# Second layer: squares behind the roundings, a tile's eight transpositions in one run, residual terms last in the second product; the weight conversion quiet in more ticks

## The chip, the cores and the metric

The kernel runs on one core of a Trainium2 chip. The metric is device time in microseconds (us) of one execution. Names of engines are those of the profile: PE (matmul) with PEld (its weight loads), DVE (vector), ACT (scalar), POOL (GpSimd), SP (whose queue starts the DMAs).

## The reference

Three layers follow one another. Attention over 2 batches x 8 heads x 768 tokens x 64 (a local window of 96 and 8 global keys, with a linear distance penalty) gives x of 1536 tokens x 512. A first layer mixes 4 experts of 512 to 1024 to 512. The second layer is the one that most of the change is in:

```python
h = x @ w_in                                  # 1536 x 1024
e = np.exp(h - np.max(h, axis=-1, keepdims=True))
sm = e / (np.sum(e, axis=-1, keepdims=True) + 1e-09)
solu = h * sm
mu = np.mean(solu, axis=-1, keepdims=True)
var = np.mean((solu - mu) ** 2, axis=-1, keepdims=True)
ln = (solu - mu) / np.sqrt(var + 1e-06) * g_ln
return ln @ w_out                             # 1536 x 512
```

All tensors are float32. The second layer's weights arrive as 64-bit words and are converted on the chip.

## The kernel before, in words

**Numbers in two halves.** A float32 value is multiplied as two parts: a rounded one (fp32r; "hi", made on ACT or POOL by a copy) and its residual ("lo", made by a subtraction on DVE or POOL). A product takes three matmuls for each 128 of depth: hi x hi, hi x lo, lo x hi.

**First layer.** `moe` goes through 8 half experts (`he`). From `he` = 2 on, one half expert is: `tail_groups` (the last 512 tokens, in seven groups of products numbered i = 1, 2, 6, 5, 7, 3, 4, of 256 columns), four groups of second products (`run`), `paired_groups` (1024 tokens, seven groups in the order 1, 2, 6, 5, 7, 4, 3, of 512 columns), and twice four groups of second products. The seven groups are a seven-product scheme for a two by two block product. In it the result of a first group is copied out of PSUM by ACT (L644 in the tail, L725 in the pairs) before the next group adds into the same bank, and DVE adds copy and bank (L652, L730) before ACT applies the ReLU (L608).

**Ticks.** Behind each group `st.tick()` writes small pieces of side work into the engines' streams: splitting of weights (L296, L304), loads, and the conversion of the second layer's weights. A conversion unit is a list of steps (`conv_steps`): load, two groups of integer operations on DVE, `two`/`both` (DVE, then the rounding on ACT, L201; for half of the units a scaling on ACT before it, L200), `parts` (L204) and a store to `w_dram` (L425). Units of the first 16 also make sums of quarter matrices and round and store those (`form`, L432 to L435: rounding on ACT, residual on DVE or POOL). With `quiet=True` a tick does no conversion step. Every engine takes its stream strictly in the order written, so a conversion step that waits holds back what stands behind it on its engine.

**Second layer.** `solu_layer` works on 12 tiles of 128 tokens. Tiles 0 and 1 get their hidden values by `g3`, the pairs after that by `pair(p)`, which again is seven groups of six matmuls in the order 1, 5, 6, 3, 7, 2, 4, with copies on ACT behind 1, 5 and 6 (L967; group 6 adds into the bank that group 1 was copied from) and additions on DVE (L970) behind 3, 7 and 2. Then come, for each tile: `largest` (DVE, L979), `powers` (ACT, L984), `products` (DVE, L989 to L994), and `squares` (ACT, L998, then two small POOL operations, L999 and L1000, that give the factor `rstd` for the output). The result must be turned so that its 1024 values lie across partitions: for tiles 0, 1, 10 and 11 by PE (`turned`: eight 128 x 128 transpositions, L1037; roundings on ACT, L1039; residuals on DVE, L1040), for the others by DVE and a trip through DRAM (`blocks`, `rounded`, `rests`). `g4(t)` is the second product, 24 matmuls in the order hi, hi, lo for each of eight slices (L1053), and its copy out (L1058) goes to `out`. Two PSUM tiles "o" are used in turn by `g4` and by `turned` for tiles 0 and 1; for tiles 10 and 11 `turned` uses the two halves of one tile.

The order of all of this is the order in which the Python code writes it; there is no planner, and the waits on semaphores follow from the data.

Of the kernel before, what the change touches and what calls it, by code (L numbers as in the profile page):

```python
# [25 lines left out]
NSLOT = NT // 128  # L26
# [25 lines left out]
def kernel(ctx, tc, ep, qk, vp, nn, pr, wall, w64, gl, out):  # L52
    nc = tc.nc
# [154 lines left out]
    def stream(arm):  # L208
# [5 lines left out]
        st = St()  # L214
# [179 lines left out]
        def conv_steps():  # L394

            n = st.next_conv
            st.next_conv += 1
            c, role, (j, h) = n, -1, (0, 0)
            if n < 16:
                role, (j, h) = n % 4, divmod(n // 4, 2)  # L400
                c = 2 * (2 * j + (1, 0, 5, 4)[role]) + h
            raw = st.cvp.tile([128, 256], I64, tag="r64", name=f"{arm}r64", bufs=2)
            af, cf = (st.cvs[:, n % 2, 256 * i:256 * i + 256] for i in range(2))
            one, two, parts, halves = from_f64(raw, af, cf)
            k0, k1 = (st.kk[:, i] for i in range(2))
            v = nc.vector

            def load():
                nc.sync.dma_start(out=raw, in_=w64[c])

            def both():
                two(gt[:, (c - 16) // 2:(c - 16) // 2 + 1] if c >= 16 else None)
                if role == 0:
                    nc.scalar.copy(k0, af)
                elif role == 1:
                    v.tensor_tensor(out=cf, in0=k0, in1=af, op=ALU.subtract)
                    nc.scalar.copy(k1, cf)
                elif role == 2:
                    v.tensor_tensor(out=cf, in0=af, in1=k0, op=ALU.subtract)
                    v.tensor_tensor(out=k1, in0=af, in1=k1, op=ALU.subtract)  # L420
                elif role == 3:
                    v.tensor_tensor(out=cf, in0=af, in1=k1, op=ALU.subtract)

            def store(p, h):
                nc.sync.dma_start(out=w_dram[p, :, :, 256 * h:256 * h + 256], in_=halves.bitcast(F32))  # L425
                st.stored += 1

            def ends():
                parts()
                store(c // 2, c % 2)  # L430

            def form(m, t, eng):  # L432
                nc.scalar.copy(halves[:, 0], t)
                eng.tensor_tensor(out=halves[:, 1], in0=t, in1=halves[:, 0].bitcast(F32), op=ALU.subtract)
                store(16 + 2 * m + j, h)  # L435

            forms = {1: [(0, cf, v)], 2: [(2, cf, v)], 3: [(3, cf, v), (1, k1, nc.gpsimd)]}.get(role, ())
            steps = [load, nothing, one, both, ends]
            for x in forms:
                steps += [nothing, lambda x=x: form(*x)]  # L440
            return n % 2, steps
# [358 lines left out]
    def moe(st, first_blocks):  # L800
# [28 lines left out]
        for he in range(1, NHE):  # L829
            if he == 1:  # L830
                yield from run(he, (2 * HALF, 512), False)
                st.tail_forms(st.now + 1)
            else:
                h3 = [], []
                for i in st.tail_groups(he, h3):
                    yield 0, 0.0
                    if i in (2, 5, 3, 4):
                        st.tick(i == 2, i != 2, 1)
                yield from run(he, (2 * HALF, 512), False, h3)
            h1, h2 = ([[None] * 4, [None] * 4] for _ in range(2))  # L840
            for i in st.paired_groups(he, h1, h2):
                yield 0, 0.0
                st.tick(quiet=i == 7)
            yield from run(he, (0, HALF), False, h1)
            yield from run(he, (HALF, HALF), True, h2)

# [23 lines left out]
    def solu_layer(st, arm):  # L870
# [13 lines left out]
        with ExitStack() as es:  # L884
# [127 lines left out]
            def halves(t, g):  # L1012
                return [x[:, g] for x in sets[t % 2]]
# [16 lines left out]

            def turned(t, pts):
                tt = t_b[t % 2]
                for g in range(2):
                    pt = pts(g)
                    for c in range(4):
                        f0 = (4 * g + c) * 128
                        nc.tensor.transpose(pt[:, 128 * c:128 * c + 128], tt[:, f0:f0 + 128], ident)  # L1037
                    th, tl = halves(t, g)
                    nc.scalar.copy(th, pt)  # L1039
                    nc.vector.tensor_tensor(out=tl, in0=pt, in1=th.bitcast(F32), op=ALU.subtract)  # L1040
                tts[t] = [[x.rearrange("p (c q) -> p c q", c=4) for x in halves(t, g)] for g in range(2)]

# [3 lines left out]
            def g4(t, f0=0, f1=8, c0=0, n=512):  # L1046
                if f0 == 0:
                    outs[t] = out_bank(t)[:, :n]
                ps = outs[t]
                for fc in range(f0, f1):  # L1050
                    th, tl = tts[t][fc // 4]
                    for i, (a, b) in enumerate(((th, 0), (th, 1), (tl, 0))):
                        nc.tensor.matmul(ps, lhsT=a[:, fc % 4], rhs=wo[fc][:, b, c0:c0 + n],  # L1053
                                         start=(fc == 0 and i == 0), stop=(fc == 7 and i == 2))
                if f1 < 8:
                    return
                o = o_b[t % 2][:, c0:c0 + n]
                nc.scalar.activation(o, ps, AF.Copy, scale=rstd[t])  # L1058
                b, i = SLOTS[t]
                nc.sync.dma_start(out=out[b * S + 128 * i:b * S + 128 * i + 128, c0:c0 + n], in_=o)  # L1060
# [3 lines left out]
            def soft_pair(p, old=None):  # L1064
                t0, t1 = 2 * p, 2 * p + 1
                largest(t0)
                powers(t0)
                if old is not None:
                    rounded(old)
                largest(t1)  # L1070
                powers(t1)
                for t in (t0, t1):
                    products(t)
                    if t == t0 and old is not None:
                        rests(old)
                    squares(t)
                    if p < last:
                        blocks(t)

            forms(1)  # L1080
            for t in range(2):
                g3(t)
                largest(t)
                powers(t)
                products(t)
                squares(t)
            load_form(3)
            forms(2)
            turned(0, out_bank)
            pair(1, {7: [lambda: turned(1, out_bank)]})  # L1090
            soft_pair(1)
            for p in range(1, last):
                if p + 2 <= last:
# [2 lines left out]
                g4(2 * p - 1)  # L1096
                pair(p + 1, {7: [lambda: rounded(2 * p), lambda: rests(2 * p)]})
                soft_pair(p + 1, 2 * p + 1)
            tail = bank()
            g4(NSLOT - 4)  # L1100
            turned(NSLOT - 2, lambda g: tail[:, g])
            g4(NSLOT - 3)
            g4(NSLOT - 2, 0, 4)
            tail = bank()
            turned(NSLOT - 1, lambda g: tail[:, g])
            g4(NSLOT - 2, 4, 8)
            g4(NSLOT - 1, 0, 8, 0, 256)
            g4(NSLOT - 1, 0, 8, 256, 256)
# [599 lines left out]
```

## Time and profile before

| | us |
|---|---|
| median of 3 runs | 752.25 |
| the runs | 752.08 to 753.03 |
| the profiled execution | 752.41 |
| its span | 750.6 |
| PE busy in the span | 723.8 (96%) |
| DVE, POOL, ACT busy | 494.3, 317.2, 311.0 |

The profile shows one execution. A row of the timeline gives the start, the busy time, the engine, the line, the operation with output and input tile, the count, and in square brackets how long the engine sat idle before it and who ended that wait. The span starts at 0; the second layer begins at 598 us. A matmul's busy time is modelled and overlaps the next; the distance between starts is what one costs.

### The profile page before, as it was taken

What the parts mean: (1) busy time and instruction counts of PE and PEld (TensorE: products, weight loads), DVE (VectorE), ACT (ScalarE), POOL (GpSimd) and SP (SyncE); (2) the same over time, 40 slices, a digit from 0 to 9 for tenths busy, and PEclk for the clock granted to TensorE, in tenths of its full rate; (3) what the DMA queues carried; (4) which work ended last, traced back from release to release, by engine and by line L of the source; (5) the groups of instructions that cost most, each with busy time, mean ns of one, the idle gap of its engine ahead of it and who ended that gap; (6) DMA issues with size and microseconds to landing.
All of it is one profiled execution on the core that took longest, in us unless ns stands there. A gap on an engine that the chain in (4) does not pass through costs nothing.

```text
span 750.6 us, 11200 instructions
## 1 busy us (share of the span) xinstructions
PE 723.8 (96%) x3887; PEld 599.6 (80%) x3887; DVE 494.3 (66%) x1083; ACT 311.0 (41%) x707; POOL 317.2 (42%) x378
## 2 busy tenths in 40 slices
PE   8999999999999999999999999999999979999966
PEld 6687877888788788889888888888988868778755
DVE  6787867638776776677769579677435546666640
ACT  4776756423522433233243253424324233444431
POOL 5600034574873074255226306422741484666000
PEclk9999999999999999999999999999999999999989
DMA  6733421312433234134143333323104840344401
GB/s 215 186 101 108 121 67 43 99 56 84 141 113 98 93 105 127 56 128 120 63 141 103 95 98 116 111 88 94 57 18 181 311 178 35 107 140 141 141 15 48
DMA packets 56979, 81.44 MB, mean 108 GB/s; under 512 B 5840, under 2 KB 34768, under 8 KB 56912
## 3 DMA queue, kind: packets, MB, share of 16 engines
q1 hardware_dynamic: 56352, 80.19, 33.7%
q8 instruction: 33, 0.54, 0.3%
q10 hardware_dynamic: 560, 0.43, 0.2%
q14 instruction: 34, 0.28, 0.1%
HBM read 60.65 MB, written 19.95 MB: 107 GB/s over the span
## 4 chain that ended last, share of the span: by engine, by line
PE 79%; DVE 11%; ACT 4%; issue 3%; DMA 1%; POOL 1%; DVEq 0%; ACTq 0%; SPq 0%; POOLq 0%
PE fg L570 34%; PE fg L720 15%; PE fg L639 6%; PE fo L1053 6%; PE fg L541 5%; PE fh L963 5%; PE x L1287 2%; PE sps L1183 2%; PE pt L1265 2%; DVE fhl L1028 1%; DVE scr L991 1%; ACT fhh L608 1%; DVE fg L652 1%; DVE fnm L979 1%; DMA v<-in_vp_dram 1%
## 5 line engine op out<-in xcount | busy, mean ns | idle before, releaser
L570 PE MATMUL fg<-fhh,wV 128*128 128x512 f32 (+1 forms) x800 | 243.5, 384 | 0.4
L570 PEld LDWEIGHTS fg<-fhh,wV 128*128 128x128 f32 x800 | 148.3, 188 | 33.7 <-issue 3.3
L570 PE MATMUL fg<-fhl,wV 128*128 128x512 f32 (+1 forms) x400 | 149.3, 381 | 0.0
L570 PEld LDWEIGHTS fg<-fhl,wV 128*128 128x128 f32 x400 | 75.0, 188 | 14.7 <-DVE fhl L556 0.3
L608 ACT ACTIVATE fhh<-fg 128x512 fp32r<-128x512 f32 x80 | 47.7, 599 | 66.3 <-DVE fg L730 36.5
L304 POOL TENSOR_TENSOR wR<-kr,wR 128x512 fp32r<-128x512 f32 (+1 forms) x28 | 29.0, 1060 | 79.7 <-ACT wR L296 79.7
L578 DVE TENSOR_TENSOR fg<-fg,pb 128x512 f32<-128x512 f32 x60 | 41.7, 694 | 28.0 <-PE fg L570 28.0
L720 PE MATMUL fg<-xt,fwS 128*128 128x512 f32 x252 | 58.3, 389 | 0.0
L583 POOL TENSOR_TENSOR scr<-scr,kr 128x512 f32<-128x512 f32 x24 | 31.0, 1292 | 61.7 <-DVE kr L582 61.7
L609 DVE SCALAR_TENSOR_TENSOR fhl<-fg,fhh 128x512 fp32r<-128x512 f32 x80 | 53.9, 687 | 3.4 <-ACT fhh L608 1.8
L720 PE MATMUL fg<-xh,wR 128*128 128x512 f32 x168 | 54.3, 391 | 1.3 <-DVE fg L730 1.3
L720 PEld LDWEIGHTS fg<-xt,fwS 128*128 128x128 f32 x252 | 47.3, 188 | 9.8
L730 DVE TENSOR_TENSOR fg<-kr,fg 128x512 f32<-128x512 f32 x42 | 28.7, 693 | 28.0 <-PE fg L720 20.9
L1053 PE MATMUL fo<-xt,fhh 128*128 128x512 f32 (+1 forms) x156 | 46.8, 385 | 0.0
L1243 ACT ACTIVATE p<-p,mn 128x256 f32<-128x256 f32 x68 | 33.8, 498 | 27.4 <-DVE mn L1238 27.4
L579 DVE TENSOR_TENSOR scr<-fg,scr 128x512 f32<-128x512 f32 x60 | 41.5, 692 | 2.0
L541 PE MATMUL fg<-xh,wR 128*128 128x512 f32 (+1 forms) x128 | 39.5, 373 | 0.0
L201 ACT CAST fr<-fcvs 128x256 fp32r<-128x256 f32 x32 | 11.9, 373 | 65.5 <-DVE fcvs L197 60.5
L720 PEld LDWEIGHTS fg<-xh,wR 128*128 128x128 f32 x168 | 31.5, 188 | 8.7 <-DVE fg L730 2.2
L582 DVE TENSOR_TENSOR kr<-fg,pb 128x512 f32<-128x512 f32 x24 | 16.6, 691 | 29.6 <-PE fg L570 27.8
L304 POOL TENSOR_TENSOR fwS<-kr,fwS 128x512 fp32r<-128x512 f32 x28 | 35.7, 1296 | 0.7 <-ACT fwS L296 0.7
L1053 PEld LDWEIGHTS fo<-xt,fhh 128*128 128x128 f32 x156 | 29.5, 196 | 5.4
(270 smaller groups left out, 1545.7 us busy)
## 6 DMA issues: line engine op xcount, KB each, us to landing
w_dram<-fr SPq DMA_DIRECT2D x48, 256.0 KB, 2.4
kr<-in_wall_dram SPq DMA_DIRECT2D x42, 256.0 KB, 2.8
fr<-in_w_dram SPq DMA_DIRECT2D x32, 256.0 KB, 2.7
pb<-p_dram SPq DMA_DIRECT2D x22, 256.0 KB, 3.7
v<-in_vp_dram SPq DMA_DIRECT2D x10, 512.0 KB, 3.5
kr<-t_dram SPq DMA_DIRECT2D x32, 128.0 KB, 2.9
frawt<-in_wall_dram SPq DMA_DIRECT2D x14, 256.0 KB, 2.8
wR<-w_dram SPq DMA_DIRECT2D x6, 512.0 KB, 4.0
```

Source lines behind the costliest of these rows:

```text
L304: e.tensor_tensor(out=w[:, 1], in0=t, in1=w[:, 0].bitcast(F32), op=ALU.subtract)
L541: nc.tensor.matmul(ps[:, :n], lhsT=w[:, a, k], rhs=b[:, k, cols], start=(k == 0 and i == 0), stop=(k == 3 and i == 2))
L570: nc.tensor.matmul(ps[:, :n], lhsT=w[:, a, k], rhs=b[k], start=(i == 0), stop=(i == 11))
L578: nc.vector.tensor_tensor(out=ps[:, :n], in0=ps[:, :n], in1=pg, op=ALU.mult)
L579: nc.vector.tensor_tensor(out=a, in0=ps[:, :n], in1=a, op=ALU.add)
L608: nc.scalar.activation(th, src, AF.Relu)
L609: residuals.append(lambda: nc.vector.scalar_tensor_tensor(out=tl, in0=src, scalar=0.0, in1=th.bitcast(F32), op0=ALU.max, op1=ALU.subtract))
L639: nc.tensor.matmul(ps[:, q_ * q:q_ * q + q_], lhsT=w[:, a, j], rhs=x[b][j], start=(opens and q == j == m == 0), stop=(j == 1 and m == 2), ...
L720: nc.tensor.matmul(ps, lhsT=w[:, a, j], rhs=x[b][j], start=(i in (1, 2, 5) and j == 0 and m == 0), stop=(j == 1 and m == 2), skip_group_ch ...
L963: nc.tensor.matmul(ps[i], lhsT=left[i][x][j], rhs=right[i][j][:, y], start=(i in (1, 5, 2) and j == m == 0), stop=(j == 1 and m == 2), ski ...
L1053: nc.tensor.matmul(ps, lhsT=a[:, fc % 4], rhs=wo[fc][:, b, c0:c0 + n], start=(fc == 0 and i == 0), stop=(fc == 7 and i == 2))
L1243: nc.scalar.activation(p[:, a], p[:, a], AF.Exp, bias=mn[:, a:a + 1], scale=-1.0, accum_out=st_rs[u][:, a, 0:1])
```

## The change

Six edits, of which none alters what is computed.

1. `form` rounds on the engine that also makes the residual (DVE for 12 of the 16, POOL for 4) and not on ACT.
2. `tail_groups`: the tick behind group 2 is quiet too (the three others were already). `paired_groups`: the tick behind group 5 is quiet as well as the one behind group 7.
3. `turned` writes its eight transpositions in one run and then both roundings; the residuals are a function of their own, `turned_rests`.
4. `g4` takes the 16 matmuls with hi on the left first and then the 8 with lo.
5. The beginning of the second layer is written in another order: roundings of tile 0 come before the exponentials of tile 1, and the squares of tiles 0 and 1 stand behind groups 3 and 7 of the first pair.
6. In the last pair `squares` goes behind the roundings of its tile.

```diff
             def form(m, t, eng):
-                nc.scalar.copy(halves[:, 0], t)
+                eng.tensor_copy(out=halves[:, 0], in_=t)
...
                     if i in (2, 5, 3, 4):
-                        st.tick(i == 2, i != 2, 1)
+                        st.tick(i == 2, True, 1)
...
-                st.tick(quiet=i == 7)
+                st.tick(quiet=i in (5, 7))
...
             def turned(t, pts):
                 tt = t_b[t % 2]
-                for g in range(2):
-                    pt = pts(g)
-                    for c in range(4):
-                        f0 = (4 * g + c) * 128
-                        nc.tensor.transpose(pt[:, 128 * c:128 * c + 128], tt[:, f0:f0 + 128], ident)
+                both = [pts(g) for g in range(2)]
+                for f in range(8):
+                    nc.tensor.transpose(both[f // 4][:, 128 * (f % 4):128 * (f % 4) + 128], tt[:, 128 * f:128 * f + 128],
+                                        ident)
+                for g, pt in enumerate(both):
+                    nc.scalar.copy(halves(t, g)[0], pt)
+                return both
+
+            def turned_rests(t, both):
+                for g, pt in enumerate(both):
                     th, tl = halves(t, g)
-                    nc.scalar.copy(th, pt)
                     nc.vector.tensor_tensor(out=tl, in0=pt, in1=th.bitcast(F32), op=ALU.subtract)
...
-                for fc in range(f0, f1):
-                    th, tl = tts[t][fc // 4]
-                    for i, (a, b) in enumerate(((th, 0), (th, 1), (tl, 0))):
-                        nc.tensor.matmul(ps, lhsT=a[:, fc % 4], rhs=wo[fc][:, b, c0:c0 + n],
-                                         start=(fc == 0 and i == 0), stop=(fc == 7 and i == 2))
+                terms = [(fc, i) for k in ((0, 1), (2,)) for fc in range(f0, f1) for i in k]
+                for fc, i in terms:
+                    a = tts[t][fc // 4][i // 2]
+                    nc.tensor.matmul(ps, lhsT=a[:, fc % 4], rhs=wo[fc][:, i % 2, c0:c0 + n],
+                                     start=(fc == i == 0), stop=(fc == 7 and i == 2))
...
                     products(t)
                     if t == t0 and old is not None:
                         rests(old)
-                    squares(t)
                     if p < last:
+                        squares(t)
                         blocks(t)
...
-            for t in range(2):
-                g3(t)
-                largest(t)
-                powers(t)
-                products(t)
-                squares(t)
+            g3(0)
+            largest(0)
+            powers(0)
+            products(0)
+            g3(1)
             load_form(3)
             forms(2)
-            turned(0, out_bank)
-            pair(1, {7: [lambda: turned(1, out_bank)]})
+            pt0 = turned(0, out_bank)
+            largest(1)
+            powers(1)
+            turned_rests(0, pt0)
+            products(1)
+            pair(1, {3: [lambda: squares(0)],
+                     7: [lambda: turned_rests(1, turned(1, out_bank)), lambda: squares(1)]})
...
-            tail = bank()
             g4(NSLOT - 4)
-            turned(NSLOT - 2, lambda g: tail[:, g])
-            g4(NSLOT - 3)
-            g4(NSLOT - 2, 0, 4)
-            tail = bank()
-            turned(NSLOT - 1, lambda g: tail[:, g])
+            t = NSLOT - 2
+            for k in range(2):
+                tail = bank()
+                turned_rests(t + k, turned(t + k, lambda g: tail[:, g]))
+                squares(t + k)
+                if k == 0:
+                    g4(NSLOT - 3)
+                    g4(t, 0, 4)
```

What stands in the engines' streams changes at three places that matter for what follows. On ACT, inside a `tail_groups` of the first layer (L644 copies a group's result out, L608 is the ReLU, L296 splits weights, L433, L201 and L417 are conversion), this stands in a row before:

```order
L296 CAST wV<-frawt 128x512
L201 CAST fr_2462<-fcvs 128x256
L417 COPY fkk<-fcvs 128x256
L644 COPY kr<-fg 128x512
L608 ACTIVATE fhh<-fg 128x512
L296 CAST wV<-kr 128x512
L644 COPY kr<-fg 128x512 x2
```

and now, at the same half expert:

```order
L296 CAST wV<-frawt 128x512
L644 COPY kr<-fg 128x512
L608 ACTIVATE fhh<-fg 128x512
L296 CAST wV<-kr 128x512
L644 COPY kr<-fg 128x512 x2
```

The conversion steps have gone from in front of the copies here; they stand elsewhere in the stream. On ACT at the start of the second layer (L984 is `powers`, L998 `squares`, L967 the copies of the pair's groups 1, 5 and 6), this stands in a row before:

```order
L984 ACTIVATE scr,fsu<-fh_5720,fnm 128x1024
L998 ACTIVATE scr,fva<-scr 128x1024
L984 ACTIVATE scr,fsu<-fh_5760,fnm 128x1024
L998 ACTIVATE scr,fva<-scr 128x1024
L1039 CAST fhh<-fo 128x512 x2
L967 COPY keep<-fh_5832 128x512
L967 COPY keep<-fh_5833 128x512
L967 COPY frawt<-fh_5832 128x512
```

and now (L1038 is the rounding of the turned tile, L1039 before):

```order
L984 ACTIVATE scr,fsu<-fh_5720,fnm 128x1024
L1038 CAST fhh<-fo 128x512 x2
L984 ACTIVATE scr,fsu<-fh_5755,fnm 128x1024
L967 COPY keep<-fh_5822 128x512
L967 COPY keep<-fh_5823 128x512
L967 COPY frawt<-fh_5822 128x512
L998 ACTIVATE scr,fva<-scr 128x1024
L1038 CAST fhh<-fo 128x512 x2
```

Both squares have moved from in front of the roundings and copies to behind the three copies. On ACT at the end of the second layer (from the exponentials of tile 11 on; L1058 is the copy out of `g4`), this stands in a row before:

```order
L984 ACTIVATE scr,fsu<-fh_6502,fnm 128x1024
L998 ACTIVATE scr,fva<-scr 128x1024 x2
L1058 ACTIVATE scr<-fo,frs 128x512
L1039 CAST fhh<-fh_6590 128x512 x2
L1058 ACTIVATE scr<-fo,frs 128x512
L1039 CAST fhh<-fh_6670 128x512 x2
```

and now (L1062 is the copy out):

```order
L984 ACTIVATE scr,fsu<-fh_6502,fnm 128x1024
L1062 ACTIVATE scr<-fo,frs 128x512
L1038 CAST fhh<-fh_6607 128x512 x2
L998 ACTIVATE scr,fva<-scr 128x1024
L1062 ACTIVATE scr<-fo,frs 128x512
L1038 CAST fhh<-fh_6665 128x512 x2
L998 ACTIVATE scr,fva<-scr 128x1024
```

Here each of the two squares has moved behind the two roundings of its own tile.

## Rows read from the trace of the kernel before

**Rows 1.** Page: busy us (share of the span) xinstructions of each engine.
```profile
PE 723.8 (96%) x3887; PEld 599.6 (80%) x3887; DVE 494.3 (66%) x1083; ACT 311.0 (41%) x707; POOL 317.2 (42%) x378
```

**Rows 2.** Chain that ended last: start us, us, what; runs of matmuls.
```profile
231.62 11.22 PE fg L570 x48
...
410.24 5.76 PE fg L639 x48
...
484.32 11.17 PE fg L570 x48
...
546.42 11.22 PE fg L570 x48
...
617.59 6.72 PE fh L963 x18
624.31 0.87 PE fo L1037 x8
...
627.94 10.88 PE fo L1053 x48
...
659.88 6.81 PE fh L963 x30
...
680.98 6.81 PE fh L963 x30
```

**Rows 3.** Timeline, first layer: PE's waits at 194 and 417 us, ACT before the latter.
```profile
193.99 0.50 PE L720 MATMUL fg<-xh,wR 128*128 128x512 f32 x1 [1.12 <-DVE fg L730]
...
415.22 0.51 ACT L200 ACTIVATE fcvs<-fr,gt 128x256 f32<-128x256 f32 x1
...
415.76 0.37 ACT L201 CAST fr<-fcvs 128x256 fp32r<-128x256 f32 x1
416.03 1.08 ACT L644 COPY kr<-fg 128x512 f32<-128x512 f32 x2
...
416.67 1.10 PE L639 MATMUL fg<-wR,fwS 128*128 128x256 f32 x7 [0.69 <-ACT kr L644]
```

**Rows 4.** Line L434, durations min/median/max ns: the residual behind the rounding that moves.
```profile
L434 DVE TENSOR_TENSOR fr<-fcvs,fr x12: 414/421/425, 181.3 to 373.8; 128x256 fp32r<-128x256 f32 x12
```

**Rows 5.** Timeline, start of the second layer, all engines.
```profile
610.79 1.12 ACT L984 ACTIVATE scr<-fh,fnm 128x1024 f32<-128x1024 f32 x1
...
612.01 1.52 PE L963 MATMUL fh<-wV,fx 128*128 128x512 f32 x6
...
614.04 0.75 DVE L994 TENSOR_SCALAR scr<-scr,fmu 128x1024 f32<-128x1024 f32 x1
614.89 1.06 ACT L998 ACTIVATE scr<-scr 128x1024 f32<-128x1024 f32 x1 [2.89 <-DVE scr L994]
...
616.89 1.08 ACT L967 COPY keep<-fh 128x512 f32<-128x512 f32 x2
...
617.59 1.62 PE L963 MATMUL fh<-fhh,fx 128*128 128x512 f32 x3 [4.06 <-POOL frs L1000]
```

**Rows 6.** Stretch 613 to 623: busy us of each engine, granted clock, DMA.
```profile
613.00:623.00 10.00, 5.94 (x17) 4.40 (x16) 3.02 (x6) 3.67 (x7) 8.01 (x14) 0.66 0.01 2
```

**Rows 7.** Timeline, second layer's steady part: PE's wait in `g4`.
```profile
654.59 0.50 PE L1053 MATMUL fo<-xt,fhl 128*128 128x512 f32 x1 [0.37 <-DVE fhl L1028]
```

**Rows 8.** Timeline, end of the second layer.
```profile
716.85 0.60 PE L1037 MATMUL fh<-ident,scr 128*128 128x128 f32 x4
...
720.49 1.06 ACT L998 ACTIVATE scr<-scr 128x1024 f32<-128x1024 f32 x1 [2.62 <-DVE scr L994]
...
723.47 1.11 PE L1037 MATMUL fh<-ident,scr 128*128 128x128 f32 x4 [6.02 <-DVE fhl L1040]
...
745.68 0.47 ACT L1058 ACTIVATE scr<-fo,frs 128x256 f32<-128x256 f32 x1 [2.26 <-PE fo L1053]
```

**Rows 9.** Timeline of SP's queue: last store of converted weights, first loads of them.
```profile
519.67 0.53 SPq L425 DMA_DIRECT2D w_dram<-fr  x1
...
561.75 12.56 SPq L263 DMA_DIRECT2D wR<-w_dram  x4
```

## The prediction

> **What bounds the kernel now.** The page comes first: PE is busy for 723.8 of a span of 750.6 us, while no other engine is over 494.3 [rows 1]. So the kernel ends when PE's stream ends, and an edit is worth what it takes out of PE's waits (plus what a wait costs behind itself). The chain of waits comes second, because it gives the starts of the long matmul runs, and from these the pace of an undisturbed PE: 48 matmuls of 512 columns in 10.88 us are 0.2267 us each, 48 of 256 columns in 5.76 us are 0.120, eight transpositions take 0.87 [rows 2]. Wherever a stretch takes longer than its count times this pace, PE lost time. Third are PE's own waits in the timeline: five in the first layer between 0.22 and 1.13 us, of which two are shown [rows 3], one of 4.06 us at 617 [rows 5], three of 0.37 us or like it in the steady part of the second layer [rows 7], and one of 6.02 us followed by 1.40 us at the end [rows 8]. The windows come last: after the wait of 4.06 us the granted clock averages 0.66 over 613 to 623 [rows 6], so a long wait is paid twice.
>
> **Term A, first layer: the quiet ticks and the roundings that leave ACT.** From the first matmul run of one half expert's tail to that of the next is one period of the same work. Six such starts lie between 231.62 and 546.42, so five periods take 314.80; the last of them, which has no wait, takes 546.42 - 484.32 = 62.10 [rows 2]. Five of those would be 310.50: 4.30 us are lost in the waits at 257, 291, 417 and 480. The wait at 194 stands before them and is 1.12 us, about 1.28 with the gap that a matmul's modelled end hides (0.39 shown for 0.23 of pace, hence 0.16). Together 5.58 us.
>
> Why they go: in the tail, ACT does a scaling of 0.51 and a rounding of 0.37 for the conversion immediately before the copy of group 6, the copy starts at 416.03, and PE, which needs it before group 7, starts 0.69 late [rows 3]. These steps were written by the tick behind group 2, which is quiet now; without 0.8 us of them the copy is done before PE asks. In the pairs, DVE makes conversion steps between groups 5 and 7, so that the addition behind group 7 comes late and group 4 waits 1.12 [rows 3]; that tick is quiet too. Moving the rounding in `form` takes 12 short operations from ACT to DVE. No DVE rounding of this size is in the trace; its nearest row is the residual that follows it, 0.42 us [rows 4], and I bound it by 0 and twice that. At 0.42 it is 5 us in all on an engine that idles over 250, and it spares DVE the wait for ACT, so I cost it at nothing; what hides it is PE's matmul run of 10.9 us behind each tick group, and without that cover it would be 5 us. The four on POOL are hidden by its idle 58%.
>
> What is late next: the conversion steps are not gone, they come in other ticks, and up to 13 ticks later. Ticks behind groups 1, 2, 6, 4 and of `run` carried such steps in every half expert before without a wait of PE. Bounds: a gain of 5.6 if all waits go, a loss of 2 if each of six half experts gets a new wait of a third of a microsecond more than it loses. I take 4.8, near the upper row, because one or two small waits may reappear.
>
> **Term B, first pair of the second layer.** Group 5 starts at 612.01, and group 6 should follow six matmuls later, at 613.37. It starts at 617.59 [rows 5]. The profile names POOL's `rstd` as what ended the wait, but group 6 adds into the bank from which ACT copies group 1, and that copy starts at 616.89, because ACT's stream had the squares of tile 1 (start 614.89, waiting for DVE's L994 of 614.04 to 614.79) and two roundings in front of it [rows 5]. The new order on ACT is roundings of tile 0, exponentials of tile 1, then the copies. The eight transpositions start at about 612.01 - 1.36 - 0.87 = 609.8; two roundings of the length of the copies (1.08 for two) end by 611.8; the exponentials (1.12) by 612.9; the first copy by 613.5 [rows 5]. So PE waits 0.1 to 0.2 instead of 4.2.
>
> From 612.01 to the transpositions of tile 1 are 24 matmuls, 5.44 us; the chain has them at 624.31 [rows 2], 12.3 us after. The difference is 6.86; of that 4.2 is the wait, and 6.72 for 18 matmuls instead of 4.08 is the clock behind it. Taking off 0.2 for the copy and 0.2 for the rougher edge of the chain's start, I book 6.5. DVE is not late next: `products` of tile 1 begins with the exponentials one microsecond later than before, so it ends near 615.8, and PE transposes its result at 617.5. The squares now stand behind PE's need; their two POOL operations go behind `forms(2)`, which starts 3 us earlier for it. Bounds: 0 (the wait is not ACT's order) and 6.9.
>
> A rule of the Trainium skill bears on that last move. The DVE subtraction of the mean took 0.75 us at 614.04 [rows 5], when POOL made only tiny operations. The page "SBUF — State Buffer" states that POOL and some DVE modes share one port pair and that the later of the two is fully blocked. By it this operation, now beside `forms(2)`, would be up to one POOL operation longer and the slack above of 1.7 us smaller; the sum stays.
>
> **Term C, `g4` with the residual terms last.** In the steady part a pair's cycle takes 680.98 - 659.88 = 21.10 us, for 42 + 48 matmuls, 20.40 at the pace [rows 2]. The excess of 0.70 is the wait for a residual on DVE [rows 7], 0.37 plus the hidden edges. With 16 hi matmuls in front, the residual has 3.6 us more, and the rounding it needs instead was made before it on ACT. Three cycles have this wait: 3 x 0.65 = 1.95. Bounds: 0 and 2.1. The number of matmuls and weight loads stays.
>
> **Term D, the end.** PE starts the transpositions of tile 10 at 716.85, stands for 6.02 us between the fourth and the fifth, and the last copy out starts at 745.68 [rows 8]: 28.83 us. The second four wait for the residual of the first four, since both halves are one tile; that residual waits for its rounding, and ACT had the squares of tile 11 (start 720.49, after a wait of 2.62 for DVE) in front of it [rows 8]. Now all eight stand before any reader. At the pace: 0.87, 36 matmuls 8.16, 0.87, 12 matmuls 2.72, 48 of 256 columns 5.76, and 0.2 to the copy: 18.6. The rest of 10.2 is 6.0 and 1.4 of waits and about 2.5 of reduced clock. What is late next: roundings of tile 10 end near 719, residuals after `products` of tile 11 (done before 720.5, when its squares start) near 722; PE asks for them at 718 + 5.4 and 3.6 later for tile 11's. Each has over a microsecond of room. Bounds: 6.0 (only the long wait goes) and 10.3.
>
> **Sum.** 4.8 + 6.5 + 1.95 + 10.2 = 23.45. From the profiled execution's 752.41 that leaves 728.96, of which 1.8 lie outside the span and stay. That execution is 0.16 above the median of 752.25, so on the median's footing 728.8; I say 729.
>
> **Rivals.**
> Quiet ticks only move the waits: A is 0, time 733.8. For it: the conversion's DVE work is unchanged and falls on other groups; against: those groups took it without a wait.
>
> The wait at 617 is POOL's or a load's, as the profile's row says [rows 5]: B is 0, time 735.5. Against: PE goes on 0.7 us after the copies start, one copy's length.
>
> The clock falls all the same at one of the two places with transpositions: 6.72 - 4.08 = 2.6 more [rows 2], time 731.6. Against: eight in a row at 624.31 took 0.87 and the following matmuls kept their pace. In the Trainium skill, "TensorE: Matmul & The Clock Gate", part 4 on PE-mode transpose, says that a transposition does not count as PE work in the way a matmul does; this speaks against putting eight in one run, and the trace so far does not bear it out.
>
> Slower than before: the conversion ends so late that the second layer's weights miss PE. The last store stands at 519.67 and the first load at 561.75 [rows 9]; SP's queue is strictly in order, so a late store holds all loads behind it. PE needs the first of them at 598 and the eight tiles take about 12 us to arrive (the first four issues alone spread over 12.56, [rows 9]), so delay begins with a store after 586, and each further microsecond costs one; it outweighs 23.4 only from 609 on. Thirteen ticks at about 2 us put the store near 550. Time if it happened: over 752.
>
> **How the numbers follow.** Forecast 0.72, with its own range of 727.6 to 731; clock 0.08; moved waits 0.11; POOL or load 0.05; slower 0.02; the other 0.02 is no change, in which the waits are all replaced. What a measurement can tell from no change here is about 0.2%, 1.5 us. The four cases on the fast side give faster 0.96; same 0.02; slower 0.02. The range reaches from all upper bounds together (5.6 + 6.9 + 2.1 + 10.3 = 24.9, 727.4) to the middle of the lost-term cases, 734.5.
>
> **What would show it.** Right: no wait of PE over 0.3 us between 190 and 600; group 6 of the first pair right behind group 5; cycles of 20.4 us; eight transpositions without a gap at the end; granted clock 1.00 in both stretches. Wrong: a wait on L644 or L730 elsewhere in the first layer (A), PE idle before group 6 with the copy done (B), PE waiting for a rounding in `g4` (C, D), a store to the weights' buffer behind 586.

## The result and the profile after

The changed kernel takes 728.88 us (median of 4 runs, 728.68 to 729.17), beside 752.49 for the kernel before: a ratio of 0.9686, 95% interval 0.9669 to 0.9703, so 23.6 us less. Forecast were 729.0 us and a gain of 23.45. The profiled execution has a span of 726.9 us (750.6 before).

The page's first part shows what is left for such edits:

```profile
PE 716.7 (99%) x3887; PEld 596.2 (82%) x3887; DVE 498.5 (69%) x1095; ACT 306.5 (42%) x691; POOL 318.8 (44%) x382
```

PE issues the same 3887 matmuls as in [rows 1], in a span that is 3% shorter.

The chain of waits gives the same landmarks as [rows 2] (start us, us, what):

```profile
230.86 11.18 PE fg L570 x48
...
479.26 11.18 PE fg L570 x48
...
541.36 11.18 PE fg L570 x48
...
605.68 6.85 PE fh L963 x30
612.53 0.87 PE fo L1035 x8
...
627.02 9.52 PE fh L963 x42
...
647.42 9.72 PE fh L963 x42
...
668.02 9.52 PE fh L963 x42
...
688.42 2.72 PE fh L963 x12
691.17 7.07 PE fh L963 x30
```

And the timeline of the end, as in [rows 8] (in square brackets the idle time before a row and who ended it):

```profile
703.52 1.04 PE L1035 MATMUL fh<-ident,scr 128*128 128x128 f32 x8
...
722.14 0.47 ACT L1062 ACTIVATE scr<-fo,frs 128x256 f32<-128x256 f32 x1 [2.27 <-PE fo L1057]
```

Subtract landmark from landmark, and each term's stretch stands by itself (times in us):

| landmark | before | after | saved up to here | this term | booked |
|---|---|---|---|---|---|
| last tail run of the first layer | 546.42 | 541.36 | 5.06 | A 5.06 | 4.8 |
| transpositions of tile 1 | 624.31 | 612.53 | 11.78 | B 6.72 | 6.5 |
| transpositions of tile 10 | 716.85 | 703.52 | 13.33 | C 1.55 | 1.95 |
| last copy out | 745.68 | 722.14 | 23.54 | D 10.21 | 10.2 |

The five periods between 230.86 and 541.36 are 62.10 us each. The granted clock is the share of its full speed that PE was given; the stretch that had 0.66 in [rows 6], a mean over the two levels of the clock, now has 1.00, the upper one, throughout (start:end, length, busy us of PE, PEld, DVE, ACT, POOL, clock, DMA share, GB/s):

```profile
605.00:612.00 7.00, 7.00 (x36) 5.87 (x34) 5.34 (x10) 4.88 (x9) 6.40 (x11) 1.00 0.16 61
```

### The profile page after: what moved, and what is told of

It reads as the page before. It is cut to its first block, busy times and chain, and to the rows that moved or that the text cites. A ratio compares the mean times of both kernels' runs of the same rounds, so it can differ in the third digit from the quotient of the medians.

```text
span 726.9 us, 11203 instructions
## 1 busy us (share of the span) xinstructions
PE 716.7 (99%) x3887; PEld 596.2 (82%) x3887; DVE 498.5 (69%) x1095; ACT 306.5 (42%) x691; POOL 318.8 (44%) x382
## 4 chain that ended last, share of the span: by engine, by line
PE 85%; POOL 4%; DVE 4%; ACT 3%; issue 2%; DMA 1%; DVEq 0%; POOLq 0%; ACTq 0%; SPq 0%
PE fg L570 35%; PE fg L720 16%; PE fo L1057 9%; PE fg L639 7%; PE fh L963 7%; PE fg L541 4%; PE x L1297 2%; PE sps L1193 2%; PE pt L1275 2%; POOL kr L664 1%; PE wp L1380 1%; DMA v<-in_vp_dram 1%; POOL frawt L664 1%; DVE fg L652 1%; ACT fhh L608 1%
## 5 line engine op out<-in xcount | busy, mean ns | idle before, releaser
L608 ACT ACTIVATE fhh<-fg 128x512 fp32r<-128x512 f32 x80 | 47.5, 597 | 64.4 <-DVE fg L730 38.2
L609 DVE SCALAR_TENSOR_TENSOR fhl<-fg,fhh 128x512 fp32r<-128x512 f32 x80 | 54.0, 686 | 7.2 <-ACT fhh L608 5.6
L730 DVE TENSOR_TENSOR fg<-kr,fg 128x512 f32<-128x512 f32 x42 | 29.0, 693 | 34.4 <-PE fg L720 24.0
L1057 PE MATMUL fo<-xt,fhh 128*128 128x512 f32 (+1 forms) x156 | 35.3, 374 | 0.0
L725 ACT COPY kr<-fg 128x512 f32<-128x512 f32 x42 | 24.1, 591 | 25.1 <-PE fg L720 25.0
L720 PE MATMUL fg<-xl,wR 128*128 128x512 f32 x84 | 32.7, 389 | 0.0
L1057 PEld LDWEIGHTS fo<-xt,fhh 128*128 128x128 f32 x156 | 27.7, 188 | 5.1
```

The costliest lines, as they stand in the source:

```text
L608: nc.scalar.activation(th, src, AF.Relu)
L609: residuals.append(lambda: nc.vector.scalar_tensor_tensor(out=tl, in0=src, scalar=0.0, in1=th.bitcast(F32), op0=ALU.max, op1=ALU.subtract))
L720: nc.tensor.matmul(ps, lhsT=w[:, a, j], rhs=x[b][j], start=(i in (1, 2, 5) and j == 0 and m == 0), stop=(j == 1 and m == 2), skip_group_ch ...
L1057: nc.tensor.matmul(ps, lhsT=a[:, fc % 4], rhs=wo[fc][:, i % 2, c0:c0 + n], start=(fc == i == 0), stop=(fc == 7 and i == 2))
```

## The experiments

Each kernel is the changed one with one thing altered (in one case two); times are medians, ratios are taken to runs of the kernel before on the same chip. Those medians of the kernel before go from 751.7 to 752.5 us, so two medians of this section that differ by less than about 0.8 us aren't told apart by their times. Spans, and landmarks within a span, are those of the profiled execution (span 726.9 for the changed kernel) and are read from one execution each.

**The quiet ticks alone undone.** (A loud tick is one that is not quiet: it does conversion steps.)

```
-                        st.tick(i == 2, True, 1)
+                        st.tick(i == 2, i != 2, 1)
-                st.tick(quiet=i in (5, 7))
+                st.tick(quiet=i == 7)
```

> The changed kernel with the conversion loud again behind group 2 of the tail and group 5 of the pairs; everything else as changed. If the conversion steps in front of ACT's copies and of DVE's additions made the first layer's waits (term A), the waits near 257, 291, 417 and 480 us come back, five periods take 313 to 315 us instead of 310.5, and the time is 732.0 to 733.5. If moving the rounding in form off ACT was what removed them, the periods stay at 62.10 and the time at 728.9 plus or minus 0.5.

Measured: 733.56 us (ratio 0.976, 0.9747 to 0.9773), span 731.4; the time is 0.06 over the expected range, the five periods take 314.57, as expected. The tail at 416 reads as in [rows 3] again, a scaling and a rounding in front of the copy, and PE late by the same 0.69:

```profile
414.63 0.50 ACT L200 ACTIVATE fcvs<-fr,gt 128x256 f32<-128x256 f32 x1
415.17 0.37 ACT L201 CAST fr<-fcvs 128x256 fp32r<-128x256 f32 x1
415.43 1.08 ACT L644 COPY kr<-fg 128x512 f32<-128x512 f32 x2
416.08 1.70 PE L639 MATMUL fg<-wR,fwS 128*128 128x256 f32 x12 [0.69 <-ACT kr L644]
```

Nearly all of term A is the ticks: 4.5 us of the 5.06 come back. The other 0.5 is edit 1. In the first layer this run differs from the kernel before by edit 1 alone, and two waits are shorter than before: 0.64 in place of 1.12 at 194, 0.86 in place of 1.13 at 291. Before, ACT had a rounding of `form` (L433) right in front of the copy that PE waits for at 291,

```profile
290.36 0.38 ACT L433 CAST fr<-fcvs 128x256 fp32r<-128x256 f32 x1
...
291.28 1.70 PE L639 MATMUL fg<-wR,fwS 128*128 128x256 f32 x12 [1.13 <-ACT kr L644]
```

and in this run it is not there:

```profile
290.61 1.70 PE L639 MATMUL fg<-wR,fwS 128*128 128x256 f32 x12 [0.86 <-ACT kr L644]
```

**The rounding in `form` alone back on ACT.**

```
-                eng.tensor_copy(out=halves[:, 0], in_=t)
+                nc.scalar.copy(halves[:, 0], t)
```

> The changed kernel with the rounding in form back on ACT. The prediction costs this edit at nothing: 728.9 plus or minus 0.4, no new wait of PE over 0.3 us. The rival, that ACT's roundings (twelve of about 0.28 us, plus DVE's wait for each) were part of the first layer's waits: 729.5 to 731, with waits on L644 or L730 between 180 and 375 us.

Measured: 728.56 us (0.9693, 0.968 to 0.9706), span 726.3. The time is in the first range, and no wait comes back; but one goes, which neither case has. The times don't tell it from the changed kernel, the rows do. The changed kernel's timeline (DVE, ACT, POOL, and PE's only wait in this layer):

```profile
181.32 0.41 DVE L433 CAST fr<-fcvs 128x256 fp32r<-128x256 f32 x1
...
183.65 0.37 ACT L201 CAST fr<-fcvs 128x256 fp32r<-128x256 f32 x1 [7.88 <-DVE fcvs L197]
...
187.48 0.74 POOL L670 TENSOR_TENSOR fx<-kr,fx 128x256 fp32r<-128x256 f32 x1 [10.04 <-ACT fx L667]
...
200.94 0.50 PE L570 MATMUL fg<-fhl,wV 128*128 128x512 f32 x1 [0.17 <-DVE fhl L609]
```

and the same steps with the rounding on ACT:

```profile
183.09 0.37 ACT L201 CAST fr<-fcvs 128x256 fp32r<-128x256 f32 x1 [2.63 <-DVE fcvs L197]
...
186.92 0.74 POOL L670 TENSOR_TENSOR fx<-kr,fx 128x256 fp32r<-128x256 f32 x1 [9.55 <-ACT fx L667]
```

DVE's extra 0.41 us stands in front of three conversion steps, ACT's rounding L201, DVE's addition L730, ACT's L667, a row of POOL operations and, behind these on ACT and DVE, the residual (L609) that PE waits for at 200.94; these start 0.5 to 0.7 later. On ACT the rounding ran beside DVE's addition of 179.9. From the first run of 48 products at 135.5 to the transpositions of tile 0 the run saves 0.49 us. So edit 1, which gave 0.5 beside loud ticks, costs about 0.5 beside quiet ones.

**The squares of tiles 0 and 1 alone in front of the first pair.**

```
+            squares(0)
+            squares(1)
-            pair(1, {3: [lambda: squares(0)],
-                     7: [..., lambda: squares(1)]})
+            pair(1, {7: [...]})
```

> The changed kernel with both squares of tiles 0 and 1 in front of the first pair, so that on ACT they stand behind the roundings and the exponentials but ahead of the three copies. If ACT's order makes the wait (term B): squares of tile 1 need DVE's subtraction, which ends at 610.4, so ACT's first copy starts near 611.5, group 6 starts near 612.2 instead of 608.3, and with the reduced clock behind the wait the time is 733 to 735.5. If the wait was POOL's, or came from the roundings alone: group 6 stays near 608.3 and the time is 728.9 plus or minus 0.5.

Measured: 734.70 us (0.9773, 0.9759 to 0.9786), span 732.6.

```profile
610.54 1.06 ACT L998 ACTIVATE scr<-scr 128x1024 f32<-128x1024 f32 x1 [2.00 <-DVE scr L994]
...
611.09 0.40 POOL L919 CAST xh<-kr 128x256 fp32r<-128x256 f32 x1
...
611.60 1.05 ACT L967 COPY keep<-fh 128x512 f32<-128x512 f32 x2
...
612.26 1.13 PE L963 MATMUL fh<-fhh,fx 128*128 128x512 f32 x2 [3.77 <-POOL xh L919]
...
619.90 0.19 POOL L999 TENSOR_SCALAR fva<-fva 128x1 f32<-128x1 f32 x1
```

Group 6 starts 0.06 us from where it was expected. The row again names POOL, but the operation that it names was over at 611.49, 0.8 us earlier, and makes an input of the next pair; the first of ACT's two copies ends at 612.17, 0.1 before PE goes on. (Before, POOL's `rstd` was over at 616.96, the first copy at 617.49, and PE went on at 617.59.) The POOL operations that belong to `squares` come only at 619.90 here, so they are not the cause. 3.8 us of wait and 1.9 behind it (18 matmuls in 5.96 us in place of 4.08) are 5.7 of term B.

**The exponentials of tile 1 alone in front of tile 0's roundings.**

```
-            pt0 = turned(0, out_bank)
             largest(1)
             powers(1)
+            pt0 = turned(0, out_bank)
```

> The changed kernel with the row maximum and the exponentials of tile 1 in front of the roundings of tile 0 again; the squares stay behind. If only the squares mattered for term B: the exponentials run from 605.7 to 606.8, the roundings to 608.0, the first copy ends at 608.6, and group 6 starts near 608.7 instead of 608.3: 729.3 to 729.6. If the roundings' place matters as much as the squares': group 6 after 610 and 731 or more.

Measured: 729.15 us (0.9698, 0.9685 to 0.9712), span 727.4. That is just under the first range; group 6 starts at 608.53 and the transpositions of tile 1 come 0.3 us later than in the changed kernel, counted from those of tile 0. By itself this part is worth about 0.3 us by the trace, too little for the times; most of term B is the squares.

**The second product's terms as before.**

```
-                terms = [(fc, i) for k in ((0, 1), (2,)) for fc in range(f0, f1) for i in k]
+                terms = [(fc, i) for fc in range(f0, f1) for i in range(3)]
```

> The changed kernel with the second product's terms again as hi, hi, lo for each slice. By term C the wait for the residual on DVE comes back three times in the steady part, 0.65 us each: 730.8, and cycles of 21.0 instead of 20.4 to 20.6. At the end a fourth and a fifth use of a residual come earlier as well, with slack of over a microsecond by the prediction: no wait there. If the order of the terms is worth nothing once the squares have moved: 728.9 plus or minus 0.4. If the end loses its slack too: over 732.

Measured: 730.46 us (0.9717, 0.9704 to 0.973), span 728.6. The chain has

```profile
648.22 6.82 PE fh L963 x30
...
669.28 6.82 PE fh L963 x30
...
690.34 9.52 PE fh L963 x42
```

so cycles of 21.06, 0.66 over the pace, and the timeline has the wait of [rows 7] again:

```profile
642.91 0.50 PE L1057 MATMUL fo<-xt,fhl 128*128 128x512 f32 x1 [0.36 <-DVE fhl L1028]
```

Three times 0.66 are 1.98, but the spans differ by 1.7, of which 0.1 lies ahead of the second layer: the stops of 0.20 and 0.27 that the changed kernel has inside its pairs (at 650 and 691, below) are gone here, since PE reaches those pairs later. The end kept its slack, as expected.

**The split of the transpositions alone, at the end.**

```
-                turned_rests(t + k, turned(t + k, lambda g: tail[:, g]))
+                (four transpositions, rounding, residual, twice)
                 squares(t + k)
```

> The changed kernel, but for tiles 10 and 11 the transpositions are again written as four, rounding, residual, four; the squares stay behind the roundings. If the split is what costs (half of term D's wait and more): the first residual of tile 10 stands behind the products of tile 11 on DVE, near 707.1 to 707.7, so the second four start at 707.8 instead of 704.0, and for tile 11 a rounding and a residual, 1.3 us, lie bare: 5 us, and up to 2.6 of reduced clock behind the first: 733.5 to 736.5. If the squares alone made the wait: 728.9 to 730.2, which is two bare round trips at most.

Measured: 736.19 us (0.9785, 0.9772 to 0.9799), span 734.3.

```profile
706.61 0.75 DVE L994 TENSOR_SCALAR scr<-scr,fmu 128x1024 f32<-128x1024 f32 x1
707.28 0.68 DVE L1056 TENSOR_TENSOR fhl<-fh,fhh 128x512 fp32r<-128x512 f32 x1
708.01 1.07 PE L1053 MATMUL fh<-ident,scr 128*128 128x128 f32 x4 [3.62 <-DVE fhl L1056]
```

The residual waits on DVE for `products` of tile 11, and PE for the residual. Of the 7.4 us of span, 5.1 are two waits (3.6 and 1.5) and 1.8 the clock behind the first (0.86 granted over 704 to 716): four transpositions take 1.07 in place of 0.44 and the 36 products 9.37 in place of 8.19. The rest, 0.5, lies ahead of the end and in the gaps that the modelled ends hide. So the end is 7.1 longer than in the changed kernel; about 3 us of term D stay without the unsplit run, and moving the squares is the likely cause of them (edit 4 wasn't taken out together with the split).

**The squares of tiles 10 and 11 alone in front of the roundings.**

```
+                    squares(t)
                     if p < last:
-                        squares(t)
                         blocks(t)
...
-                squares(t + k)
```

> The changed kernel, but the squares of tiles 10 and 11 stand behind their products again, ahead of the roundings; the eight transpositions stay in one run. If the split was the cause: the roundings of tile 10 come 4 us later, near 708.2 to 709.3, the first products of the tile that use them start at 709.9 and the residuals are wanted at 711.7: 728.9 to 729.8. If the squares are the cause: PE waits for a rounding or residual of tile 10 by 3 us or more, 732 to 735.

Measured: 728.88 us (0.9692, 0.9679 to 0.9705), span 727.0, against 726.9. ACT does tile 10's roundings only at 708.86, 4.2 us later than in the changed kernel, and PE does not notice:

```profile
703.74 0.87 PE fh L1035 x8
704.61 8.18 PE fo L1057 x36
712.79 0.87 PE fh L1035 x8
713.66 8.51 PE fo L1057 x60
```

Edit 6 is worth nothing beside edit 3; with edits 3 and 4 in place all of term D is there without it.

**Each transposition of tiles 10 and 11 four times.**

```
-                for f in range(8):
+                for f in [f for f in range(8) for _ in range(4 if t >= NSLOT - 2 else 1)]:
```

> The changed kernel with each transposition of tiles 10 and 11 written four times in a row, 32 in place of 8 for each tile, into the same place. If a transposition costs its own time alone: 48 more at 0.109 us, 5.2 us, 734.1, and the granted clock stays 1.00. If a run of transpositions is too little work to keep the clock: 2.6 us more behind one run or behind both, 736.7 to 739.3, with a granted clock under 0.9 over the microseconds behind the run.

Measured: 734.45 us (0.9763, 0.9749 to 0.9776), span 732.6: 5.7 more than the changed kernel, 5.24 of it the transpositions (3.49 in place of 0.87, twice) and 0.4 ahead of the second layer's first transposition. The 36 products behind take 8.21 in place of 8.19: no clock is lost.

**Each transposition of tile 10 sixteen times** (16 and `t == NSLOT - 2` in the same line).

> The changed kernel with each transposition of tile 10 written sixteen times, 128 in place of 8. If a transposition keeps the clock as a product does: 120 more at 0.109 us, 13.1 us, 742.0, granted clock 1.00 throughout. If a long run of them lets the clock fall: each of the later ones takes twice as long, up to 13 us more, and the products behind start at the lower clock: 745 to 757.

Measured: 742.01 us (0.9868, 0.9852 to 0.9883), span 740.2. The chain, and below it two stretches (columns as above):

```profile
703.91 13.97 PE fh L1035 x128
717.88 8.18 PE fo L1057 x36
```

```profile
703.00:718.00 15.00, 15.00 (x134) 14.75 (x134) 4.17 (x9) 0.71 (x2) 0.00 (x0) 1.00 0.05 19
718.00:726.00 8.00, 8.00 (x37) 6.58 (x36) 1.29 (x2) 2.78 (x5) 0.74 (x2) 1.00 0.09 33
```

128 transpositions take 0.109 us each from the first to the last, with a granted clock of 1.00 in them and behind them.

**The squares of the steady pairs moved too.** What the changed kernel has in front of one of its two stops in the pairs:

```profile
688.25 1.06 ACT L998 ACTIVATE scr<-scr 128x1024 f32<-128x1024 f32 x1 [3.74 <-DVE scr L994]
...
689.31 1.25 ACT L1062 ACTIVATE scr<-fo,frs 128x512 f32<-128x512 f32 x2
...
690.45 1.31 ACT L967 COPY keep<-fh 128x512 f32<-128x512 f32 x2
...
691.17 0.70 PE L963 MATMUL fh<-fhh,xh 128*128 128x512 f32 x2
```

```
                     if p < last:
-                        squares(t)
+                        if t == t0:
+                            squares(t)
...
-                pair(p + 1, {7: [...]})
+                pair(p + 1, {6: [lambda: squares(2 * p + 1)], 7: [...]})
```

> The changed kernel, and in the steady pairs too the squares of the second tile move: behind group 6 of the next pair instead of in front of that pair's copies on ACT. If ACT's squares in front of the copies make the two remaining small waits of PE in the pairs (0.2 us at 650.0 and 0.27 at 691.2): all cycles 20.40 and 728.3 to 728.5, a difference too small for the times but not for the spans (726.4 against 726.9). If something else makes them: spans stay at 726.9. If the squares then come too late for the copies out: over 729.

Measured: 728.49 us (0.9687, 0.9674 to 0.97), span 727.1. All cycles are 20.40 (pairs at 627.70, 648.10, 668.50 and 688.90), so the stops were ACT's order. The span did not fall as expected, because in this execution the work before the first run of 48 products ended 0.6 us later; from the transpositions of tile 0 to the end it saves 0.5. Spans of the changed kernel's own runs go from 726.9 to 727.3.

**Both together:** the steady squares moved and `form` rounding on ACT.

> The changed kernel with the rounding in form back on ACT, and the squares of the steady pairs' second tiles behind group 6 of the next pair. If the two gains seen apart are separate (0.57 us in the first layer, where DVE's rounding delays a chain over ACT and POOL to PE near 200 us, and 0.48 in the pairs): span 725.8 to 725.9, time 727.6 to 728.1. If they are chance: span 726.9, time 728.9.

Measured: 727.94 us (0.9682, 0.9669 to 0.9696), span 726.0, as expected to 0.1. From the first run of 48 products (135.6 in both) to the transpositions of tile 0 it saves 0.51, in the second layer 0.51 more. It is the lowest median of the study; its interval and the changed kernel's overlap, so that it is faster is read from the traces, not from the ratios. Beside the run above, which differs from it by the rounding in `form` alone, it has the shorter span in every run (five from 725.9 to 726.6, five from 726.7 to 727.3, on another chip).

**The conversion late.**

```
-                if (st.rest >= 2 and st.formed and ...
+                if (st.rest >= (2 if st.next_conv < 26 else 6) and st.formed and ...
```

> The changed kernel with the last six conversion units started at least six loud ticks apart, so that the last ones are written in the ticks after the first layer's last products. The last store is expected at 598 to 602 us. By the rival as the prediction has it (a store past 586 holds all the loads behind it, each further microsecond costs one): 741 to 745. If only the loads of the late pieces wait, which are the last ones that PE asks for (group 5 of the first pair, at 606.9): PE waits a few us there, 729 to 734.

Measured: 756.12 us (1.0053, 1.0038 to 1.0069), span 754.8. 0.5% slower than the kernel before, and both expectations missed. The last store is far later than I thought, and it is not the loads that PE waits for:

```profile
617.70 0.42 DVE L204 TENSOR_TENSOR fr<-fcvs,fr 128x256 fp32r<-128x256 f32 x1 [0.96 <-ACT fr L201]
```

```profile
570.06 2.04 SPq L263 DMA_DIRECT2D wR<-w_dram  x4
...
618.15 0.52 SPq L425 DMA_DIRECT2D w_dram<-fr  x1
```

```profile
618.18 1.22 PE L942 MATMUL fh<-wR,xh 128*128 128x512 f32 x2 [24.64 <-DVE fr L204]
```

The first loads were issued at 570; some of a later piece are issued behind the last store, at 620.71, and PE never waits for them. PE's first product of the second layer, which in the changed kernel starts at 593.17, waits for DVE's last reading of `fcvs`. That tile and the second layer's first PSUM tile have the same tag in a pool with one buffer (L856, L901 of the kernel), and PE starts 0.06 us after that reading ends. So by the row and the code the second layer begins when the last conversion step is done.

## Why the prediction was right, point by point

**What bounds it.** Right: a PE time line with known pace, on which each wait could be priced. Spans fell by 23.7, the four terms add up to 23.54. That the sum came out within 0.1 us of the booked 23.45 is in part luck: A and B were booked 0.5 too low together, C 0.4 too high.

**Term A.** Booked 4.8 with an upper bound of 5.58, measured 5.06. The ticks make 4.5 of it, edit 1 beside loud ticks the rest. The five periods gave all of their 4.30, though the four waits named for them add up to 2.7 (3.4 with 0.16 for each hidden gap): booking by the period, and not by the waits, was what kept the sum right. What fell short is the wait at 194, which gave 0.76 of the 1.28 booked at most, as a wait of 0.17 at 200.94 took its place. "I cost it at nothing", said of the roundings that leave ACT, failed in both directions: the roundings had a part in the waits at 194 and 291, and with these gone cover was there for PE's groups, but not for the chain over ACT, POOL and DVE that ends in the residual at 200.94, where 0.41 us on DVE cost 0.5. The allowance of 0.8 for "one or two small waits" happened to hold this, which is luck.

**Term B.** Booked 6.5, measured 6.72. ACT's order was the wait; the rival that took POOL for it fell with the squares alone moved back. The squares make 5.7 of it; the exponentials' place makes 0.3 by itself, and the last 0.7 comes only with both: with both as before the wait is 4.06 and not 3.77 us, and the 18 matmuls behind it take 0.76 longer. The clock's share is shown twice: 18 matmuls in 6.72 us before, 5.96 in the experiment.

The rule on the port pair that DVE and POOL share was one of two places where the Trainium skill spoke against the change: by "SBUF — State Buffer", "Who interferes with whom", a DVE operation that uses the shared pair and one of POOL fully block each other, and the one that issues first goes first. The rows agree with that as far as they go: `products` of tile 1 now stands between two POOL operations,

```profile
609.14 0.74 POOL L923 TENSOR_TENSOR kr<-xh,xl 128x256 f32<-128x256 f32 x1
...
609.50 0.93 DVE L994 TENSOR_SCALAR scr<-scr,fmu 128x1024 f32<-128x1024 f32 x1
...
609.96 1.07 POOL L924 TENSOR_TENSOR kr<-kr 128x256 f32<-128x256 f32 x1
```

against 0.75 for the same DVE line alone [rows 5] and 0.74 for POOL's. DVE starts 0.38 before the first POOL operation ends and is 0.18 longer; the second POOL operation starts 0.47 before DVE ends and is 0.33 longer. Tile 0's operation of this line starts 0.60 before a POOL operation ends and is 0.40 longer, in both kernels. So the later one loses all of the overlap but 0.14 to 0.2 us, and in the other runs this DVE line, with overlaps of 0.35 to 0.62, is longer by the overlap less 0.2 as well. The prediction's "up to one POOL operation longer" was an upper bound, well above the 0.18 that came. PE lost nothing by it: it transposes the result at 612.37, 1.9 us after DVE is done.

**Term C.** Booked 1.95, measured 1.55. The three waits were worth 0.66 each, booked 0.65. What was missed is what comes late next: with PE sooner in the pairs, ACT's squares and two copies out stand in front of the copy for group 6, 0.20 and 0.27 in two pairs. Moving those squares took it away.

**Term D.** Booked 10.2, measured 10.21. The step "that residual waits for its rounding, and ACT had the squares of tile 11 in front of it" names only a part of the cause, and by its own weight the smaller one. With the split and without those squares in front PE still waits 3.6 of the 6.0 us, because the residual also stands behind `products` of tile 11 on DVE; with the squares in front and without the split it waits for nothing.

**Rivals.** The clock near transpositions: refuted, with 128 in a row. The rule of the Trainium skill named beside it ("TensorE: Matmul & The Clock Gate", part 4 on PE-mode transpose), that a transpose-mode operation does not count as PE-busy in the same way, does not show here: the products behind 128 of them kept their pace, 8.18 for 36. Whether the matmuls against the identity that the trace shows use the mode which that page means, no run shows. The moved waits: one of 0.17 us, and the two stops of term C. The late conversion: its risk is real, but its place was wrong. Not the weights' loads but a shared PSUM tile decides, so the limit is 593, the first product of the second layer, for the last conversion step on DVE, not 586 for the last store. In the changed kernel the last conversion step is the row below, with its store at 556.00 (the prediction had the store near 550); 37 us of room were left.

```profile
555.55 0.42 DVE L204 TENSOR_TENSOR fr<-fcvs,fr 128x256 fp32r<-128x256 f32 x1 [0.96 <-ACT fr L201]
```

## What to carry to other kernels

On a kernel bound by one engine, take the pace of that engine from undisturbed runs in the chain, and price every stretch by what it lies over the pace: four terms read so came out within 0.4 us each. For each of its waits list what stands in front of the releasing instruction on that engine's stream, and move what nobody needs soon (statistics for a later scale, conversion for a later stage) behind it; where a loop alternates two engines over one tile, issue all of the first engine's part at once. And before an operation is moved to an engine because that engine is idle, look for a chain that passes through it at that moment; the same move can gain before another edit and cost after it, as edit 1 did.

## What the runs showed of the hardware

A transposition on PE here costs 0.109 us in a row of 8, 32 or 128 alike, and the granted clock is 1.00 in and behind the row of 128. A stop of PE of 3.6 to 4.1 us is followed by 1.8 to 2.6 us more at a lower clock: 2.6 in the kernel before, 1.9 with the squares in front of the pair, 1.8 with the split at the end. A DVE operation that starts while one of POOL runs, and a POOL operation that starts while that DVE operation runs, was longer by the overlap less 0.14 to 0.2 us in the rows above. And the name at the end of a row can be that of an operation long done: POOL stood there for both waits that ACT's order made, over 0.6 and 0.8 us before PE went on, while ACT's copy was over 0.1 us before.
